# Attention and spectral mixing on one core: a head in halves, GpSimd's products tied to places on VectorE, two more packs of scores off ScalarE

## The chip, the core and the metric

The kernel runs on one core of a Trainium2 chip. The core has five engines that run side by side, each with its own in-order queue: TensorE (PE in the profile, weight loads PEld), VectorE (DVE), ScalarE (ACT), GpSimd (POOL) and SyncE (SP, which here only issues DMAs). They tell each other by semaphores when a buffer is written or free. The metric is the device time of one execution in microseconds (us).

## The reference

```python
def reference(A_x, A_wqkv, A_wo, B_x, B_w_r, B_w_i, gate_w):
    x = A_x                                                # 1 x 2048 x 448, bf16
    g = _sigmoid((x * gate_w).sum(-1, keepdims=True))
    a = _A_ref(x, A_wqkv, A_wo)                            # softmax attention, 16 heads of 28
    b = _B_ref(x, B_w_r, B_w_i)                            # irfft2(rfft2(x) * (w_r + i w_i))
    return g * a + (1 - g) * b
```

Attention needs 16 x 2048 x 2048 exponentials. The two-dimensional Fourier transforms are done as matmuls with constant matrices, in stages between which the data pass through DMAs.

## The kernel before

**Work units.** Heads go in four groups T of four. Queries go in chunks of 512: chunk c = 4T + qc, 16 in all. For one chunk, 16 key tiles i of 128 rows and 4 heads make 64 score tiles of 128 x 512, 1024 in the whole kernel. A score tile is one matmul on a strip of 32 rows of TensorE (`score`, L759).

**Two ways to an exponential.** Most score tiles go to ScalarE: TensorE writes three of them into the three-bank buffer ps3 or two into ps2, alternately, and one ACTIVATE (`exp`, L951) makes the exponentials of the whole buffer. The others are taken in packs of four heads of one (c, i) by VectorE (`pack_step`, L769, and `chain`, L781). Four evictions (L775) bring the scores from a background bank bg0 or bg1 to SBUF as 16-bit whole numbers, and a chain of seven operations o1 to o7 of 128 x 2048 elements (L789 to L810) builds the bits of the exponential. There are 28 packs. `away` (L914) decides before each score tile whether a step of a pack fits; `claim` (L995) picks the pack.

**Values and chunks.** `pv` (L871, matmuls L876) multiplies exponentials with values into one accumulating bank, psPV. When a chunk is complete, `close_chunk` (L833) copies the bank (L838), sends the row of sums through DMAs (r16), takes its reciprocal (L848), multiplies by the gate (L849), writes it to DRAM (rD), and reads it back spread over the partitions (rep). Then `scale` (L863) lets GpSimd multiply: the product at L867 writes a quarter of oT[T]. There are 15 such products; the last chunk is finished in `finale`.

**Background units.** Everything else is cut into units (projections of q and k, values, the Fourier stages, output blocks), each with one or more phases: matmuls into bg0 or bg1, then VectorE's eviction. `plan` (L958) writes a list of them with due times: `first` at once, `order` at BEGIN + GAP x n. The units for group T > 0 project q and k (`qk_unit`, L493); VectorE copies a quarter (L501) and squares it (L505), and the squares are summed by head for the softmax bound (`kn_unit`, `qn_unit`).

**The order.** The program is laid out by hand: `stream` steps through exponentials and keeps an estimate of each engine's time (`tp` TensorE, `tv` VectorE, `tg` GpSimd, `ta` ScalarE, with the constants E_... at the top). Before each exponential it lets values, units and pack steps in as far as the estimate has room (`step`, L1065; `dve`, L349; `fill_v`, L817, takes chain operations from the queue `vq`). It also adds matmuls on zeros (`zero`, `dummy`, L1134 and L1143, and L909) so that TensorE stays busy. What comes out is a fixed order on each engine; nothing is decided while it runs.

**Head and tail.** `head` (L281) transposes the first block of x (L278, copies L313, L315, L316), projects k and q of its 512 columns (L270), squares them on ScalarE (L298), subtracts half the squared norm by a matmul (L303) and copies them to kT and qT (L324, L325). It also transposes and copies block 1 and half of block 2 (L321, L327, L329). `first_unit` (L534) does the other three blocks of group 0 in the stream. `finale` (L1272 on) transposes the last chunk's sums (L1291), scales (L1292 to L1294), transposes back (L1295), multiplies by Wo (L1298) and adds what was kept of the other terms, on VectorE (L755) and ScalarE (L1304), with the f32 identity matmul (L1285) where ScalarE copies.

Of the kernel before, what the change touches and what calls it, by code (L numbers as in the profile page):

```python
# [16 lines left out]
ALU = mybir.AluOpType  # L17
# [30 lines left out]
GAP = 2.3  # L48
WINDOW, PULL = 3.4, 3900
READY = 1.2  # L50
NPT = 4
# [3 lines left out]
STEPS = 3400  # L55
BEGIN = 25.0

# [87 lines left out]
class Kernel:  # L145
    def __init__(self, ctx, tc, A_x, A_wqkv, A_wo, B_w_r, B_w_i, gate_w, out):
        self.ctx, self.tc = ctx, tc
        self.nc = tc.nc
        self.x = A_x[0]
        self.wqkv, self.wo, self.w_r, self.w_i = A_wqkv, A_wo, B_w_r, B_w_i  # L150
        self.gate_w = gate_w
        self.outv = out[0].rearrange("(p t) d -> p t d", t=NT)
        self.tp = self.tv = self.tg = self.ta = self.lock = 0.0
        self.gq, self.last_v = [], None
        self.bank_free = [0.0, 0.0]
        self.vq = []
        self.events = []
        self.marks = {}
        self.active = []
        self.cols = [0, 0, 0]  # L160


    def setup(self):
# [20 lines left out]
        for b in range(4):  # L184
            nc.sync.dma_start(out=self.xtok[:, 4 * b:4 * b + 4, :], in_=xv[:, 4 * b:4 * b + 4, :])
            if b == 0:

                for part, queue in ((1, nc.scalar), (0, nc.sync)):
# [16 lines left out]
        for q in (1, 0):  # L205
# [61 lines left out]
    def project(self, ps, T, q, b, pad=True):  # L267
        for c in range(4):
# [12 lines left out]
    def head(self):  # L281

        nc, tc = self.nc, self.tc
        with tc.tile_pool(name="hps", bufs=1, space=PSUM) as hp:
            def zeros(n):
                wt = hp.tile([P, 512], F32, name="wt", tag="wt")
# [3 lines left out]
            def turn(b, c0):  # L290
                pt = banks[b, c0]
                self.transposes(pt, b, c0)
                return pt

            def proj(q):
                self.project(pk[q], 0, q, 0, False)
                sq = self.rot2.tile([P, 512], BF16, name="sqh")
                nc.scalar.activation(out=sq[:], in_=pk[q][:], func=ACT.Square)  # L298
                return pk[q], sq

            def norm(q, pk, sq):
                off = 0 if q else KR
                nc.tensor.matmul(pk[:], lhsT=self.Sel[:, off:off + P], rhs=sq[:], start=False, stop=True,  # L303
                                 skip_group_check=True)


            banks = {(2, 0): hp.tile([P, 2, 512], BF16, name="t20")}
            zeros(8)
            banks |= {(0, c): hp.tile([P, 2, 512], BF16, name=f"t0{c}") for c in (0, 2)}
            pk = [hp.tile([P, 512], F32, name=f"pk{q}") for q in (0, 1)]  # L310
            banks |= {(1, c): hp.tile([P, 2, 512], BF16, name=f"t1{c}") for c in (0, 2)}
            pt = turn(0, 0)
            nc.vector.tensor_copy(out=self.xT[0:DC, 0:2, 0:512], in_=pt[0:DC])  # L313
            pt = turn(0, 2)
            nc.scalar.copy(out=self.xT[0:DC, 2, 0:512], in_=pt[0:DC, 0])  # L315
            nc.vector.tensor_copy(out=self.xT[0:DC, 3, 0:512], in_=pt[0:DC, 1])  # L316
            zeros(4)
            k = proj(1)
            q = proj(0)
            pt = turn(1, 0)  # L320
            nc.vector.tensor_copy(out=self.xT[0:DC, 0:2, 512:1024], in_=pt[0:DC])  # L321
            norm(1, *k)
            norm(0, *q)
            nc.vector.tensor_copy(out=self.kT[0][:, 0:512], in_=k[0][:])  # L324
            nc.scalar.copy(out=self.qT[0][:, 0:512], in_=q[0][:])  # L325
            pt = turn(1, 2)
            nc.vector.tensor_copy(out=self.xT[0:DC, 2:4, 512:1024], in_=pt[0:DC])  # L327
            pt = turn(2, 0)
            nc.vector.tensor_copy(out=self.xT[0:DC, 0:2, 1024:1536], in_=pt[0:DC])  # L329
            self.tv = 1.4  # L330
# [18 lines left out]
    def dve(self, cost, fast=False, at=0.0, of=None):  # L349


        start = max(self.tv, at)
# [140 lines left out]
    def qk_unit(self, T, q, b):  # L493
# [5 lines left out]
        def ve(ps):  # L499
            dst = (self.kT if q else self.qT)[T][:, 512 * b:512 * b + 512]  # L500
            nc.vector.tensor_copy(out=dst, in_=ps[:])  # L501
            if b == 0:
                self.sq = self.rot1.tile([P, S], BF16, name="sq")
                self.marks[f"sq{T}{q}"] = self.sq
            nc.vector.tensor_tensor(out=self.sq[:, 512 * b:512 * b + 512], in0=dst, in1=dst, op=ALU.mult)  # L505
            self.marks[f"sqt{T}{q}"] = self.dve(0.46, True) + 0.1
# [27 lines left out]
    def first_unit(self, q, b):  # L534
# [4 lines left out]
        def pe(ps):  # L539
            self.project(ps, 0, q, b, False)  # L540
# [14 lines left out]
        needs = ([f"T{b}.0", f"T{b}.2"] if b > 1 else []) if q else [f"W{b}"]  # L555
        return Unit(f"{'qk'[q]}0.{b}", [(pe, 0.96, 2048, ve, 1.06), (pe2, 0.30, 512, ve2, 0.60)], needs=needs)
# [224 lines left out]
    def chain(self, c, i, t16):  # L781
        nc = self.nc
        v = nc.vector
        st = {}
# [38 lines left out]

    def at(self, t, fn):
# [8 lines left out]
    def close_chunk(self, c):  # L833
# [23 lines left out]
        def spread():  # L857
# [3 lines left out]
            self.at(self.tv + 3.0, scale)  # L861

        def scale():  # L863
# [3 lines left out]
            nc.gpsimd.tensor_tensor(out=self.oT[T][:, QW * qc:QW * qc + QW], in0=o32[:], in1=st["rep"][:], op=ALU.mult)  # L867
            self.gp(1.27, self.tp + 0.1, lambda end: self.marks.update({f"oT{c}": end + 0.1}))
# [10 lines left out]
    def scores(self, k, end):  # L879
# [3 lines left out]
        t = self.tiles[k]  # L883
        start = max(self.tp, end + AP)
# [29 lines left out]
    def away(self, start, strips):  # L914
        if len(self.vq) > 8 or self.tv > start + 1.2:
# [10 lines left out]
        ps = self.psp.tile([P, 512], F32, name=f"bg{b}", tag=f"bg{b}", bufs=1)  # L926
        if self.tv < self.tp:
# [30 lines left out]
    def plan(self):  # L958
# [10 lines left out]
        def mix(a, b):  # L969
# [13 lines left out]
        T = {2: [self.turn_unit(2, 2)], 3: [self.turn_unit(3, c) for c in (0, 2)]}  # L983
        self.marks["T2.0"] = self.tv
        first = ([self.first_unit(1, 1)] + T[2] + [self.first_unit(1, 2)] + T[3] + [self.first_unit(1, 3)]
                 + [self.ek_unit()] + W[:2] + [self.first_unit(0, 1)] + W[2:])
        order = self.gate_unit() + [self.first_unit(0, 2), self.first_unit(0, 3)]
        order += mix(V, qk(1)) + mix(fA[:26], qk(2)) + fA[26:] + mix(BI[:22], qk(3)) + BI[22:] + Z
        order += [self.base_unit(t) for t in range(8, 16)]

        m = [(0.0, u) for u in first] + [(BEGIN + GAP * n, u) for n, u in enumerate(order)]
        m += [(0.0, self.out_unit(t)) for t in range(8)] + [(0.0, self.fin_unit(t)) for t in range(8, 12)]
# [47 lines left out]
    def pick(self):  # L1040
# [4 lines left out]
        banks = [b for b in (0, 1) if b not in self.open]  # L1045
# [12 lines left out]
    def ready(self):  # L1058

        t = [self.bank_free[b] for b in self.open]  # L1060
        if len(self.open) < 2 and self.mand:
            t.append(max([self.marks.get(n, 1e9) for n in self.mand[0][1].needs] + [self.tp]))
        return min(t, default=1e9)

    def step(self, u, b, limit):  # L1065
# [5 lines left out]
        if b not in self.open:  # L1071
            self.take(u)
            self.open[b] = u, self.psp.tile([P, 512], F32, name=f"bg{b}", tag=f"bg{b}", bufs=1)
        ps = self.open[b][1]
        n = len(self.vq)
        self.fill_v(start + cost + PV - 0.3)
# [9 lines left out]
        if not u.phases:  # L1086
            del self.open[b]
            self.marks[u.name] = max(self.tv, self.tp) + u.lag
# [48 lines left out]

    def dummy(self):


        while sum(self.cols) < STEPS:
            if self.pv_open:
                self.nc.tensor.matmul(self.psPV[:], lhsT=self.warm[:], rhs=with_free(self.warm[:], [[0, 4], [1, P]]), start=False, stop=False,  # L1143
                                      skip_group_check=True)
                self.add(self.tp + E_MM, 512)
                self.dummies += 1
            elif self.pv_c < NC and self.tp >= self.pv_free:
                self.zero(self.psPV, self.tp)
            else:
                b = [i for i in (0, 1) if self.bank_free[i] <= self.tp and i not in self.open]  # L1150
                if b:
                    ps = self.psp.tile([P, 512], F32, name=f"bg{b[0]}", tag=f"bg{b[0]}", bufs=1)
# [214 lines left out]
```

## Time and profile before

| | |
|---|---|
| median of 3 runs | 439.64 us (439.36 to 439.95) |
| profiled execution | 441.74 us, span of its instructions 439.7 us |
| first exponential begins | 10.58 us |
| last exponential ends | 430.67 us |
| TensorE busy (with modelled ends) | 407.9 us, 93% |
| VectorE busy | 391.4 us, 89% |
| ScalarE busy | 419.7 us, 95% |
| GpSimd busy | 29.9 us, 7% |

A line of a group reads: line of the code, engine, operation, what it writes <- what it reads, shapes, count | busy us, mean ns of one | idle time of the engine before them and what ended it. A line of the timeline reads: start, us, engine, line, operation, count, and in brackets the idle time before it and what ended that. A line of the windows reads: stretch, its length, then for PE, PEld, DVE, ACT and POOL the busy us and the number of instructions, then the granted clock of TensorE as a share, the DMA share and GB/s. Operations of one engine overlap at their ends, so the distance of two starts is less than the duration of one.

### The profile page before, as it was taken

The numbers are of one execution on the slowest core, as the hardware profiler recorded it, in microseconds if no ns is written. First come the engines' busy times: TensorE is split into PE (matmuls) and PEld (weight loads), VectorE is DVE, ScalarE is ACT, GpSimd is POOL, SyncE is SP. The second block draws the span as 40 slices with busy tenths as digits, with TensorE's granted clock in tenths as the row PEclk, the third lists the DMA queues.
The fourth block names the chain that finished last, engine by engine and source line by source line (L and its number), as shares of the span: only waits on it lengthen the run. The fifth ranks groups of instructions, "written<-read, shape, count | busy, mean of one in ns | idle before, by whom it ended". The sixth has DMA issues, their size and how long they took to land.

```text
span 439.7 us, 8021 instructions
## 1 busy us (share of the span) xinstructions
PE 407.9 (93%) x3114; PEld 148.0 (34%) x3114; DVE 391.4 (89%) x614; ACT 419.7 (95%) x375; POOL 29.9 (7%) x33
## 2 busy tenths in 40 slices
PE   8888999999999999999999999899998899999995
PEld 4433332333333333333333333333443333333321
DVE  5686997999778999999999899999999989999953
ACT  3998998999999999999999999999999999999992
POOL 6000001100001000010110101001010101002010
PEclk9999998999999999999999999999999999999999
DMA  9900100000002010221432235024320000010111
GB/s 233 207 9 1 6 27 1 26 1 26 3 13 54 15 47 22 73 65 35 112 95 79 53 65 92 16 43 93 87 94 4 26 1 26 12 36 33 37 64 42
DMA packets 24597, 21.69 MB, mean 49 GB/s; under 512 B 10256, under 2 KB 20240, under 8 KB 24528
## 3 DMA queue, kind: packets, MB, share of 16 engines
q1 hardware_dynamic: 23808, 20.86, 19.3%
q8 instruction: 24, 0.39, 0.4%
q10 hardware_dynamic: 752, 0.33, 0.3%
q14 instruction: 13, 0.11, 0.1%
HBM read 15.36 MB, written 1.97 MB: 39 GB/s over the span
## 4 chain that ended last, share of the span: by engine, by line
ACT 38%; PE 24%; DVE 20%; issue 13%; DMA 4%; POOL 0%; SPq 0%; ACTq 0%; DVEq 0%; POOLq 0%
ACT Pt L951 38%; PE psPV L876 5%; PE ps L761 4%; DVE t L775 3%; PE bg L909 3%; PE bg L270 2%; DVE n L806 2%; PE bg L761 2%; DVE pa L800 2%; DVE pa L803 1%; DVE pa L797 1%; DMA Wv<-in_gate_w_dram 1%; PE psPV L1143 1%; DMA W<-in_A_wqkv_dram 1%; DVE U L620 1%
## 5 line engine op out<-in xcount | busy, mean ns | idle before, releaser
L951 ACT ACTIVATE Pt<-ps 128x1536 bf16<-128x1536 f32 x347 | 394.6, 1312 | 4.9 <-PE ps L761 4.6
L761 PE MATMUL ps<-qT,kT 32*128 32x512 bf16 x912 | 145.3, 382 | 10.6 <-ACT Pt L951 8.1
L876 PE MATMUL psPV<-Pt,vsb 128*32 128x512 bf16 x868 | 86.1, 388 | 0.0
L761 PEld LDWEIGHTS <-kT 32*128 32x128 bf16 x1024 | 50.3, 91 | 102.6 <-issue 95.4
L775 DVE TENSOR_SCALAR t<-bg 128x512 uint16<-128x512 f32 x112 | 76.3, 683 | 4.9 <-PE ps L761 3.9
L909 PE MATMUL bg<-warm 32*128 32x512 bf16 x145 | 55.5, 383 | 3.6 <-DVE t L775 1.3
L867 POOL TENSOR_TENSOR oT<-o,rep 128x512 bf16<-128x512 f32 x15 | 21.2, 1416 | 389.8 <-DMA rep<-rD 303.1
L761 PE MATMUL bg<-qT,kT 32*128 32x512 bf16 x112 | 42.7, 381 | 4.9 <-DVE base L741 1.1
L876 PEld LDWEIGHTS <-vsb 128*32 128x32 bf16 x1024 | 23.9, 93 | 54.8 <-issue 50.9
L806 DVE TENSOR_TENSOR n<-t,pa 128x2048 uint16<-128x2048 uint16 x28 | 36.1, 1288 | 0.4
L803 DVE TENSOR_TENSOR pa<-pa,n 128x2048 f16<-128x2048 f16 x28 | 35.5, 1267 | 0.6
L797 DVE TENSOR_TENSOR pa<-pa,n 128x2048 f16<-128x2048 f16 x28 | 34.7, 1238 | 0.1
L270 PE MATMUL bg<-xT,Wg 128*128 128x512 bf16 (+1 forms) x120 | 31.8, 388 | 0.6 <-DVE t L775 0.3
L909 PEld LDWEIGHTS <-warm 32*128 32x128 bf16 x145 | 12.3, 91 | 39.3 <-issue 38.7
L800 DVE TENSOR_SCALAR pa<-pa 128x2048 f16<-128x2048 f16 x28 | 22.9, 818 | 0.2
L620 DVE CAST U<-bg 128x450 bf16<-128x450 f32 x32 | 19.8, 621 | 2.0 <-PE bg L632 1.2
L793 DVE TENSOR_SCALAR pa<-n 128x2048 f16<-128x2048 uint16 x28 | 20.6, 737 | 0.1
L789 DVE TENSOR_SCALAR n<-t 128x2048 uint16<-128x2048 uint16 x28 | 19.7, 703 | 0.3
L810 DVE TENSOR_SCALAR Pd<-n 128x2048 uint16<-128x2048 uint16 x28 | 19.5, 696 | 0.2
L1143 PE MATMUL psPV<-warm 128*128 128x512 bf16 x58 | 19.4, 386 | 0.0
L270 PEld LDWEIGHTS <-Wg 128*128 128x128 bf16 (+1 forms) x128 | 10.9, 98 | 15.8 <-issue 7.9
L609 PE MATMUL bg<-Bd,xT 128*128 128x450 bf16 x64 | 15.0, 356 | 0.1
(159 smaller groups left out, 406.3 us busy)
## 6 DMA issues: line engine op xcount, KB each, us to landing
rep<-rD SPq DMA_DIRECT2D x15, 256.0 KB
CR<-cRB SPq DMA_DIRECT2D x8, 256.0 KB
UT<-U SPq DMA_DIRECT2D x16, 112.5 KB
VT<-U SPq DMA_DIRECT2D x16, 112.5 KB
xtok<-in_A_x_dram SPq DMA_DIRECT2D x4, 448.0 KB
CR<-cCS SPq DMA_DIRECT2D x8, 192.0 KB
Wqkv<-in_A_wqkv_dram SPq DMA_DIRECT2D x1, 1176.0 KB
Wri<-in_B_w_r_dram SPq DMA_DIRECT2D x8, 112.5 KB
```

Of the source, the lines that this page charges most:

```text
L270: self.nc.tensor.matmul(ps[:], lhsT=self.Wg[T, q][0:k, c, :], rhs=self.xT[0:k, c, 512 * b:512 * b + 512], start=(c == 0), stop=(c == 3))
L620: self.nc.vector.tensor_copy(out=U[:], in_=ps[:, 0:F2])
L761: self.nc.tensor.matmul(out, lhsT=self.kT[T][32 * h:32 * h + 32, 128 * i:128 * i + 128], rhs=self.qT[T][32 * h:32 * h + 32, QW * qc:QW * q ...
L775: nc.vector.tensor_scalar(out=pk["t"][:, h, :], in0=ps[:], scalar1=SCALE * LOG2E * 512.0, scalar2=127.0 * 512.0, op0=ALU.mult, op1=ALU.add)
L797: v.tensor_tensor(out=st["a"][:], in0=st["a"][:], in1=st["n"][:], op=ALU.mult)
L800: v.tensor_scalar(out=st["a"][:], in0=st["a"][:], scalar1=k, scalar2=C1 * k, op0=ALU.mult, op1=ALU.add)
L803: v.tensor_tensor(out=st["a"][:], in0=st["a"][:], in1=st["n"][:], op=ALU.mult)
L806: v.tensor_tensor(out=st["n"][:], in0=t16[:], in1=st["a"][:], op=ALU.add)
L876: self.nc.tensor.matmul(self.psPV[32 * h:32 * h + 32, :], lhsT=self.vsb[:, i, 4 * T + h, :], rhs=pcs[h], start=first, stop=last, tile_posi ...
L909: self.nc.tensor.matmul(ps[:], lhsT=self.warm[sl], rhs=with_free(self.warm[sl], [[0, 4], [1, P]]), start=True, stop=True, tile_position=(3 ...
L951: self.nc.scalar.activation(out=Pt[:, 0:n, :], in_=ps[:, 0:n, :], func=ACT.Exp, scale=SCALE)
L1143: self.nc.tensor.matmul(self.psPV[:], lhsT=self.warm[:], rhs=with_free(self.warm[:], [[0, 4], [1, P]]), start=False, stop=False, skip_grou ...
```

## The change

- The head works on two halves of 256 columns for q and k. All four squares are of 256 columns, three on ScalarE and one on VectorE; ScalarE copies one half of q, VectorE the other and both halves of k. VectorE makes both copies of the first block of x. Of block 1 only one half is transposed in the head, and none of block 2; the rest become units of the stream. The loads and spreadings of the first q and k weights change places.
- The order of the first units is a written list, FIRSTS; the projections of `first_unit` are two phases. Until unit W0 begins, psPV's bank serves as a third bank for units. Waits of TensorE's estimated time are filled with matmuls on zeros (`until`, `one_zero`).
- The squares of a group's q or k are one operation of 128 x 2048 at the fourth quarter, put at the front of the queue, instead of four of 128 x 512.
- A product of GpSimd is no longer issued when its estimated time comes, but put on a list, 8 us (estimated) behind the load of rep. `dve` takes it from the list when the next operation that is not of the queue, with the wait before it, is estimated at 1.0 us or more, when the queue is empty, or after 8 us. A memset by VectorE of a corner of the product's output, just ahead of that operation, holds the product until then.
- When three or fewer key tiles of the chunk under way are left, the chain operations of that chunk's packs are all done at once (`hurry`).
- GAP is 2.35 instead of 2.3; the first 8 value units are mixed with the second group's q and k, and the other 8 with the units that follow.
- In the finale the scaling and the transposing back go in two halves, three of the four blocks are copied by ScalarE, one by VectorE, and two DMAs move to SP.
- By the order of the built programs, the number of packs becomes 30 instead of 28 and the number of exponentials on ScalarE 362 instead of 365.

```diff
-GAP = 2.3
+GAP = 2.35
+BESIDE = 1.0
+NV, NBASE = 8, 8
+MOST = 8
+LATE = 3
+FIRSTS = "T1.2 k0.1 T2.0 T2.2 k0.2 T3.0 T3.2 k0.3 ek0 W0 q0.1 W1 W2 W3"
...
     def head(self):
...
-            pt = turn(0, 0)
-            nc.vector.tensor_copy(out=self.xT[0:DC, 0:2, 0:512], in_=pt[0:DC])
-            pt = turn(0, 2)
-            nc.scalar.copy(out=self.xT[0:DC, 2, 0:512], in_=pt[0:DC, 0])
-            nc.vector.tensor_copy(out=self.xT[0:DC, 3, 0:512], in_=pt[0:DC, 1])
-            zeros(4)
-            k = proj(1)
-            q = proj(0)
...
+            self.transposes(pt[0], 0, 0)
+            nc.vector.tensor_copy(out=self.xT[0:DC, 0:2, 0:512], in_=pt[0][0:DC])
+            self.transposes(pt[1], 0, 2)
+            nc.vector.tensor_copy(out=self.xT[0:DC, 2:4, 0:512], in_=pt[1][0:DC])
+            zeros(1)
+            ka = (bank("wt"), 1, 0)
+            for part in ((0, 1), (2, 3)):
+                for piece in (qa, qb, ka):
+                    proj(piece, part)
+            sa, sb = square(qa, nc.scalar), square(qb, nc.scalar)
+            proj(kb, (0, 1))
+            norm(qa, sa)
+            norm(qb, sb)
+            sk = square(ka, nc.vector)
+            proj(kb, (2, 3))
+            done(qa, nc.scalar.copy)
+            done(qb, nc.vector.tensor_copy)
+            norm(ka, sk)
+            sk = square(kb, nc.scalar)
+            done(ka, nc.vector.tensor_copy)
+            self.transposes(pt1, 1, 0)
+            norm(kb, sk)
+            nc.vector.tensor_copy(out=self.xT[0:DC, 0:2, 512:1024], in_=pt1[0:DC])
+            done(kb, nc.vector.tensor_copy)
...
     def dve(self, cost, fast=False, at=0.0, of=None):
+        if self.jobs and not fast:
+            since, job = self.jobs[0]
+            if not self.vq or max(at - self.tv, 0.0) + cost >= BESIDE or self.tv > since + 8.0:
+                self.jobs.pop(0)
+                job()
...
-            if b == 0:
-                self.sq = self.rot1.tile([P, S], BF16, name="sq")
-            nc.vector.tensor_tensor(out=self.sq[:, 512 * b:512 * b + 512], in0=dst, in1=dst, op=ALU.mult)
+            if b == 3:
+                self.vq.insert(0, (squares, E_TT, None))
...
+    def hurry(self):
+        if self.pv_c < NC and len(self.left[self.pv_c]) <= LATE:
+            self.fill_v(1e9, max((j + 1 for j, (_, _, of) in enumerate(self.vq) if of and of["c"] == self.pv_c), default=0))
...
-            self.at(self.tv + 3.0, scale)
+            self.at(self.tv + 8.0, lambda: self.jobs.append((self.tv, scale)))
...
+            nc.vector.memset(o[0:32, 0:4], 0.0)
+            nc.gpsimd.tensor_tensor(out=o, in0=o32[:], in1=st["rep"][:], op=ALU.mult)
...
-        order += mix(V, qk(1)) + mix(fA[:26], qk(2)) + fA[26:] + mix(BI[:22], qk(3)) + BI[22:] + Z
+        order += mix(V[:NV], qk(1)) + mix(V[NV:] + fA[:26], qk(2)) + fA[26:] + mix(BI[:22], qk(3)) + BI[22:] + Z
...
-        banks = [b for b in (0, 1) if b not in self.open]
+        banks = [b for b in (0, 1, 2)[:2 if self.begun else 3] if b not in self.open]
...
+    def until(self, at):
+        while self.tp + E_MM <= at and sum(self.cols) < STEPS and self.one_zero():
+            self.tp += E_MM
+        self.tp = max(self.tp, at)
...
     def finale(self, psp):
...
-        pf = [r[3][:, 0], r[3][:, 1], r[3][:, 2], r[2][:, 0]]
+        pf = [r[3][:, 0], r[3][:, 1], r[2][:, 0], r[3][:, 2]]
...
-        v.tensor_tensor(out=z[:], in0=f[:], in1=with_free(i16[:], [[1, NT], [0, 32]]), op=ALU.mult)
-        v.transpose(out=self.oT[T][:, QW * qc:QW * qc + QW], in_=z[:].rearrange("p j r -> p (j r)"))
+        for a in (0, 8):
+            zh = z[:, a:a + 8, :]
+            v.tensor_tensor(out=zh, in0=f[:, a:a + 8, :], in1=with_free(i16[:, a:a + 8], [[1, 8], [0, 32]]), op=ALU.mult)
+            v.transpose(out=self.oT[T][:, QW * qc + 32 * a:QW * qc + 32 * a + 256], in_=zh.rearrange("p j r -> p (j r)"))
+            for e in (a // 4, a // 4 + 1):
...
+        for e in (0, 1, 3):
             t = 4 * qc + e
...
+            fin = self.rot3.tile([P, F2], BF16, name="X1")
+            nc.scalar.copy(out=fin[:, 0:D], in_=pf[e][:, 0:D])
+            (nc.scalar if e == 3 else nc.sync).dma_start(out=self.outv[:, t, :], in_=fin[:, 0:D])
+        self.add_base(pf[2], 4 * qc + 2, nc.sync)
```

## The prediction

> **What bounds the kernel now.** I read the page first: busy time by engine, the clock row, the costliest groups.
>
> ```profile
> span 439.7 us, 8021 instructions
> ...
> PE 407.9 (93%) x3114; PEld 148.0 (34%) x3114; DVE 391.4 (89%) x614; ACT 419.7 (95%) x375; POOL 29.9 (7%) x33
> ...
> L951 ACT ACTIVATE Pt<-ps 128x1536 bf16<-128x1536 f32 x347 | 394.6, 1312 | 4.9 <-PE ps L761 4.6
> ```
>
> ScalarE's exponentials (L951) fill nine tenths of the span. The next view is ScalarE's timeline, merged; it shows where they do not run.
>
> ```profile
> 10.58 6.88 ACT L951 ACTIVATE early<-ps 128x1536 bf16<-128x1536 f32 x6 [0.68 <-PE ps L761]
> ...
> 39.61 2.37 ACT L951 ACTIVATE Pt<-ps 128x1536 bf16<-128x1536 f32 x2 [1.06 <-PE ps L761]
> ...
> 70.96 1.45 ACT L951 ACTIVATE Pt<-ps 128x1536 bf16<-128x1536 f32 x1 [1.34 <-PE ps L761]
> 73.12 123.61 ACT L951 ACTIVATE Pt<-ps 128x1024 bf16<-128x1024 f32 x109 [0.71 <-PE ps L761]
> ```
>
> The first exponential begins at 10.58, the last ends at 430.67, and 9.03 us of tail follow. Between, ScalarE waits four times before 43 us (0.18, 0.20, 1.06, 0.26) and twice around 70 us (1.34, 0.71); afterwards 109 of them run without a gap. So time is gained by (a) an earlier first exponential, (b) fewer of them, (c) fewer of those waits, (d) a shorter tail. What VectorE and TensorE do counts only where ScalarE waits for it.
>
> The groups with shapes kept apart give the prices.
>
> ```profile
> L951 ACT ACTIVATE Pt<-ps 128x1536 bf16<-128x1536 f32 x174 | 265.2, 1524 | 3.6 <-PE ps L761 3.6
> L951 ACT ACTIVATE Pt<-ps 128x1024 bf16<-128x1024 f32 x173 | 189.7, 1099 | 1.2 <-PE ps L761 1.0
> L800 DVE TENSOR_SCALAR pa<-pa 128x2048 f16<-128x2048 f16 x28 | 22.9, 818 | 0.2
> ```
>
> **(b) Fewer exponentials: -3.6 us.** The built order of the changed program has 120 evictions of scores to VectorE instead of 112 (30 packs, not 28), so 904 score tiles of 512 are left to ScalarE instead of 912: 173 + 8 three-wide, 170 + 10 two-wide and a single, against 174 + 8, 173 + 10. Instructions overlap, so I price by starts: 109 in 123.61 us (55 two-wide, 54 three-wide) are 2.27 us a pair. The third tile costs 1524 - 1099 = 0.425; so two-wide 0.92, three-wide 1.345, a single 0.50. 3 x 0.92 + 1.345 - 0.50 = 3.6.
>
> **What it costs VectorE.** A pack: four evictions that start 0.60 apart and seven operations whose means (703, 737, 1238, 818, 1267, 1288, 696 ns) less 0.08 overlap each sum to 6.2: 8.6 us, two are 17. Squares: 24 pieces of 0.425 go, each held up 0.08 by the copy just before; six whole ones come, of which no row exists; the nearest (L797, two half-width inputs, same size) is 1.24. 24 x 0.43 - 6 x 1.24 = 2.9 saved (0 if a whole one cost four pieces); I take 2. Fifteen small memsets at 0.06 (the row of L253): +1. Then GpSimd's products. The timeline around 66 us shows what they do now:
>
> ```profile
> 66.12 1.27 POOL L867 TENSOR_TENSOR oT<-o,rep 128x512 bf16<-128x512 f32 x1 [56.50 <-DMA rep<-rD]
> 66.31 1.62 DVE L793 TENSOR_SCALAR pa<-n 128x2048 f16<-128x2048 uint16 x1
> ...
> 68.59 1.59 PE L1134 MATMUL bg<-warm 128*128 128x512 bf16 x3 [0.46 <-DVE t L775]
> ```
>
> L793, which alone takes 0.68 (the same kind at 64.46), takes 1.62 when a product began 0.19 before it, and ends 0.54 behind it. Over the chain's groups the means exceed the undisturbed 0.68 and 1.22 by 218 and 142 ns in all, times 28: 10 us. In the changed order a product waits for a memset, and in all 15 places VectorE's next operation reads PSUM (0.6 us, in five places 1.1 or more) and only then a chain operation follows. The products come later (planned 8 us behind the issue of rep instead of 3), but each still stands ahead of the next chunk's reciprocal, so SP's next load of the single rep buffer doesn't wait for it. I count half of the 10 as gone (bounds: none, all). Net for VectorE: +17 - 2 + 1 - 5 = +11.
> [...]
>
> Is there room? By windows VectorE is busy 42.5, 49.2, 48.9, 48.1, 47.9, 47.6 us in the six 50 us stages from 100 on, and 63.7 of 72 between 28 and 100: 24 us idle from 28 to 400. With +11 some 13 are left, less the 3.6 by which the time shrinks. The packs go where room is: in the old order one eviction stands between score tiles 200 and 250, in the new one 8, since the keys and queries of the second group now mix with 8 value units, not 16. **New waits of ScalarE: +1.5 us.** Bounds: 0 (in 150 to 200 VectorE is busy 98.4% and ScalarE idle 0.30), and +2.3 if all stages came to the worst of those six (250 to 300, idle 0.55: 6 x 0.55 = 3.3 against 1.6 now, and 8/6 of the difference for 28 to 430); I take a value nearer the upper end, since every stage is now about as full as the fullest were.
>
> **(a) The head: -0.95 us.** Now, from the timeline: second half of xT copied by 6.71, eight projections 6.32 to 8.22, squares from 7.39 and 8.26 (0.60 each), copies 9.31 to 9.99, scores 10.11, exponential 10.58. In halves: VectorE's two xT copies start 5.21 and 5.81 and end 5.90 and 6.50 (no wait for ScalarE's copy). Six half-width matmuls at 0.12 (1.90/8, halved) from 5.97, six more until 7.4. ScalarE squares q from 7.1, half of 0.60 plus what is fixed, 0.38 each. VectorE takes the first keys at 7.6: copy 0.42, wait 0.1, product 0.29, to 8.3 or 8.4; norm matmul to 8.6; copy 0.42 to 9.05; scores 9.15, exponential 9.6. Behind the norm of the first keys on TensorE stand 8 transposes (0.61) and the last norm, ahead of the scores; they end about 9.15 too. Their input is there: now they run at 8.06. Bounds: -0.3 (a half as dear as a whole on VectorE: +0.7), -1.1.
>
> **(c) Early waits: -1.3 us.** The 1.06 at 38.5 is for qT of the second chunk (TensorE waits for DVE qT L554, 38.36 to 39.05). In the new order that copy stands behind two operations of the first chain and one value unit, not seven and three: some 5.7 + 1.5 us of VectorE's work come after it instead. Moved in return: transposes and copies of the second block (two of 0.69) into the stream; a third PSUM bank takes them and the next keys are wanted only 16 tiles (7.3 us) after the first exponential. Bounds: 0, -1.7.
>
> **(c) The half clock: -1.0 us.** The windows on both sides of 69.13 us:
>
> ```profile
> 65.72:69.13 3.41, 2.79 (x20) 0.88 (x20) 3.27 (x6) 3.41 (x4) 1.27 (x1) 1.00 0.00 0
> 69.13:72.54 3.41, 3.30 (x10) 0.64 (x8) 1.14 (x2) 1.94 (x2) 0.00 (x0) 0.50 0.02 2
> ```
>
> TensorE (first busy column) had 2.79 of 3.41 us, with the wait of 0.46 behind VectorE's late eviction; then its clock is 0.50 for 3.41 us and ScalarE waits 1.34 + 0.71 = 2.05. It began with the product of 66.12. With products moved I count half (0 to -2.05).
> [...]
>
> **(d) The tail: -0.5 us.**
>
> ```profile
> 433.13 0.71 DVE L1295 STREAM_TRANSPOSE oT<-oz 128x512 bf16<-128x512 bf16 x1
> ...
> 434.68 0.62 DVE L755 TENSOR_TENSOR U<-ps,late 128x448 bf16<-128x448 f32 x1 [0.84 <-PE ps L1298]
> 435.33 0.53 ACT L1304 CAST X<-ps 128x448 bf16<-128x448 f32 x1 [4.66 <-DVE U L755]
> ```
>
> Four copies alternate between two engines, each waiting for the other, 434.68 to 436.84. The halves (0.42 + 0.43 each) give the first part of oT at 433.3 but the second at 434.1, 0.25 later than now; TensorE has a third f32 matmul (0.88) for two fills fewer and is free at 433.9 either way. ScalarE's first copy waits for the last of the four matmuls (the order's semaphore values), so starts at 434.9; three copies 0.45 apart end at 436.35. Their first two DMAs go from SP (0.35 each), ahead of VectorE's. Bounds: 0, -1.0.
>
> Later places of units (GAP 2.35, out units), the hurried chains and the reversed weight loads have one answer: nothing waits for them in rows of before (q and k weights land together, 4.98 and on), 0. The last product stands 11 score tiles before the end (before: 26, at 420.75) with its four units behind it; late by 1 us it would stall the last scores by as much, inside the +1.5.
>
> Sum: -3.6 - 0.95 - 1.3 - 1.0 - 0.5 + 1.5 = -5.85. The profiled execution took 441.74 (span 439.7 and 2.0 around it), so 435.9 for its like; the median shown is 439.64, so **433.8**. A difference under 0.2% (0.9 us) can't be told from none.
>
> **Rivals.**
> A. No half clock, no early and no new wait: -3.6 - 0.95 - 1.7 - 2.05 - 0.5 = -8.8, **430.8**. For it: the causes are removed. Against: 97% of VectorE's time is taken.
> B. Products don't begin at the chosen places: a memset may run when the landing of rep has not come, and the product falls into chain operations as before. VectorE keeps its 10 us and the clock its 2.05: about +1.0 and +0.5, **435.3**. For: landing of rD has taken 3.7 us in the chain of waits; against: the product is placed 8 us behind the issue of rep.
> C. VectorE becomes the bound: both packs dearer than its idle time; ends and early waits are all that is left: **437**. Against: 24 us idle.
> D. Slower: half-clock windows. Place: the fuller stages, where a late eviction holds TensorE's queue as at 68.59. Price 2.05 each; it decides from four more than I count (-5.85 + 4 x 2.05 = +2.35): **442.0**. For: TensorE's fill matmuls fall from 237 to 230, and VectorE has less slack to catch up. Against: one in 365 us now, with worse stalls.
>
> **How the numbers follow.** Forecast 0.58 (its own range 431.8 to 436), A 0.17, B 0.11, C 0.08, D 0.06. The range 430.6 to 437.4 leaves out D and some edges of A and C. Faster: all but D and the edge of C, 0.91; within 0.2% 0.03; slower 0.06.
>
> **What would show it.** First exponential at 9.6; 362 exponentials; no gap near 38; chain operations without 1.6 to 2.2 us runs; clock row without a half window before the tail; last exponential to end of span 8.5. I am wrong if ScalarE's idle time between 100 and 400 us exceeds 3.3, if a half window stays, or if the first exponential is later than 10.2.

## The result and the profile after

The changed kernel takes 436.6 us (median of 9 runs, 434.45 to 439.07); the kernel before, beside it, 439.9 us (9 runs, 439.35 to 440.75). The ratio is 0.9926, 95% interval 0.9908 to 0.9943: faster by 0.7%, inside the range, 2.8 us above the 433.8 forecast. Its runs also spread more than before's. The profiled execution took 436.6 us. In what follows, runs that lie over 1.5% above the fastest of their kernel are left out (two of the twelve of experiment 3).

Page of the changed kernel: span, busy time, largest group.

```profile
span 434.6 us, 8031 instructions
...
PE 402.0 (93%) x3100; PEld 148.3 (34%) x3119; DVE 399.9 (92%) x638; ACT 415.4 (96%) x373; POOL 27.7 (6%) x33
...
L1002 ACT ACTIVATE Pt<-ps 128x1536 bf16<-128x1536 f32 x344 | 391.0, 1312 | 4.1 <-PE ps L798 2.7
```

VectorE gained 8.5 us (11 were forecast), ScalarE lost 4.3. An exponential is as long as before on average (1312 ns); there are 362. ScalarE's timeline, merged as before:

```profile
10.24 7.16 ACT L1002 ACTIVATE early<-ps 128x1536 bf16<-128x1536 f32 x6 [0.93 <-PE ps L798]
...
24.93 3.71 ACT L1002 ACTIVATE early<-ps 128x1536 bf16<-128x1536 f32 x3 [0.60 <-PE ps L798]
...
37.07 2.40 ACT L1002 ACTIVATE Pt<-ps 128x1536 bf16<-128x1536 f32 x2 [0.60 <-PE ps L798]
40.61 4.62 ACT L1002 ACTIVATE Pt<-ps 128x1536 bf16<-128x1536 f32 x4 [1.15 <-PE pv L923]
...
76.25 140.53 ACT L1002 ACTIVATE Pt<-ps 128x1024 bf16<-128x1024 f32 x124 [0.19 <-PE ps L798]
217.20 96.16 ACT L1002 ACTIVATE Pt<-ps 128x1024 bf16<-128x1024 f32 x85 [0.43 <-PE ps L798]
313.58 2.45 ACT L1002 ACTIVATE Pt<-ps 128x1536 bf16<-128x1536 f32 x2 [0.23 <-PE ps L798]
317.07 11.48 ACT L1002 ACTIVATE Pt<-ps 128x1536 bf16<-128x1536 f32 x10 [1.04 <-PE ps L798]
```

From 76 us on ScalarE hardly stops: 209 exponentials with one wait between them. But the first begins at 10.24, not 9.6; the early waits are 0.15, 0.60, 0.60 and 1.15 where before has 0.18, 0.20, 1.06 and 0.26; and there is again a gap that belongs to a stretch of half clock (the granted clock of TensorE is 0.50 there), now near 315 (before: near 70). Windows of the changed kernel (busy us and count of PE, PEld, DVE, ACT, POOL, then the granted clock):

```profile
310.32:313.74 3.42, 2.06 (x24) 0.58 (x22) 3.42 (x6) 3.19 (x4) 0.00 (x0) 1.00 0.15 37
313.74:317.15 3.41, 3.41 (x20) 0.83 (x17) 3.31 (x4) 2.37 (x3) 0.00 (x0) 0.50 0.45 145
```

TensorE had 2.06 of 3.42 us to do while VectorE was busy throughout; then the clock is 0.50 for 3.41 us. The tail:

```profile
428.33 0.45 DVE L1369 STREAM_TRANSPOSE oT<-oz 128x256 bf16<-128x256 bf16 x1
...
429.11 0.45 DVE L1369 STREAM_TRANSPOSE oT<-oz 128x256 bf16<-128x256 bf16 x1
430.07 0.62 DVE L792 TENSOR_TENSOR U<-ps,late 128x448 bf16<-128x448 f32 x1 [0.52 <-PE ps L1372]
```

After it ScalarE copies three blocks in one piece, 430.26 to 431.66; last exponential to end of span is 8.43 us (before 9.04).

### The profile page after: what moved, and what is told of

Its sections match the earlier page's. It is cut to its first block, busy times and chain, and to the rows that moved or that the text cites. A ratio compares the mean times of both kernels' runs of the same rounds, so it can differ in the third digit from the quotient of the medians.

```text
span 434.6 us, 8031 instructions
## 1 busy us (share of the span) xinstructions
PE 402.0 (93%) x3100; PEld 148.3 (34%) x3119; DVE 399.9 (92%) x638; ACT 415.4 (96%) x373; POOL 27.7 (6%) x33
## 4 chain that ended last, share of the span: by engine, by line
ACT 36%; PE 34%; DVE 15%; issue 12%; DMA 1%; SPq 0%; DVEq 0%; ACTq 0%
ACT Pt L1002 36%; PE psPV L923 6%; PE ps L798 5%; PE bg L959 5%; DVE t L812 3%; PE bg L276 2%; PE bg L798 2%; PE psPV L1203 2%; DVE pa L834 1%; DMA Wri<-in_B_w_i_dram 1%; PE bg L755 1%; PE bg L751 1%; DVE pa L830 1%; PE wt L297 1%; DVE kT L535 1%
## 5 line engine op out<-in xcount | busy, mean ns | idle before, releaser
L1002 ACT ACTIVATE Pt<-ps 128x1536 bf16<-128x1536 f32 x344 | 391.0, 1312 | 4.1 <-PE ps L798 2.7
L812 DVE TENSOR_SCALAR t<-bg 128x512 uint16<-128x512 f32 x120 | 82.0, 683 | 4.3 <-PE bg L798 2.1
L959 PE MATMUL bg<-warm 32*128 32x512 bf16 x150 | 57.7, 385 | 6.6 <-DVE t L812 3.4
L798 PE MATMUL bg<-qT,kT 32*128 32x512 bf16 x120 | 45.9, 383 | 2.5 <-DVE t L812 0.9
L912 POOL TENSOR_TENSOR oT<-o,rep 128x512 bf16<-128x512 f32 x15 | 19.0, 1269 | 391.7 <-DVE oT L911 299.4
L843 DVE TENSOR_TENSOR n<-t,pa 128x2048 uint16<-128x2048 uint16 x30 | 38.1, 1270 | 0.3
L834 DVE TENSOR_TENSOR pa<-pa,n 128x2048 f16<-128x2048 f16 x30 | 37.2, 1240 | 0.1
L840 DVE TENSOR_TENSOR pa<-pa,n 128x2048 f16<-128x2048 f16 x30 | 36.6, 1221 | 0.3
L276 PE MATMUL bg<-xT,Wg 128*128 128x512 bf16 (+1 forms) x98 | 28.8, 380 | 1.4 <-issue 0.3
L830 DVE TENSOR_SCALAR pa<-n 128x2048 f16<-128x2048 uint16 x30 | 21.3, 710 | 0.1
L837 DVE TENSOR_SCALAR pa<-pa 128x2048 f16<-128x2048 f16 x30 | 20.7, 690 | 0.3
L1002 ACT ACTIVATE early<-ps 128x1024 bf16<-128x1024 f32 (+1 forms) x12 | 13.9, 1209 | 1.7 <-PE ps L798 1.5
```

The source lines that it names most:

```text
L276: self.nc.tensor.matmul(ps[:], lhsT=self.Wg[T, q][0:k, c, :], rhs=self.xT[0:k, c, 512 * b:512 * b + 512], start=(c == 0), stop=(c == 3))
L798: self.nc.tensor.matmul(out, lhsT=self.kT[T][32 * h:32 * h + 32, 128 * i:128 * i + 128], rhs=self.qT[T][32 * h:32 * h + 32, QW * qc:QW * q ...
L812: nc.vector.tensor_scalar(out=pk["t"][:, h, :], in0=ps[:], scalar1=SCALE * LOG2E * 512.0, scalar2=127.0 * 512.0, op0=ALU.mult, op1=ALU.add)
L830: v.tensor_scalar(out=st["a"][:], in0=st["n"][:], scalar1=C3 * k * k, scalar2=C2 * k, op0=ALU.mult, op1=ALU.add)
L834: v.tensor_tensor(out=st["a"][:], in0=st["a"][:], in1=st["n"][:], op=ALU.mult)
L840: v.tensor_tensor(out=st["a"][:], in0=st["a"][:], in1=st["n"][:], op=ALU.mult)
```

## Theories and experiments

**H, half clock.** The gain is what was summed, 5 us, and stretches at half clock take part of it back, more often than before. **V, VectorE.** At 92% busy it is late everywhere, and the clock only shows it. Each run's mean granted clock is known, so the two can be told apart. Ratios below are to the kernel before on the same chip, with 95% intervals.

**1. The changed kernel again** (no edit).

> The changed kernel itself, once more. Theory H (half clock): what the change gained is 5.2 us (434.5 at a mean granted clock of 0.999), and each stretch of 3.41 us at half clock, which is 0.004 of the mean clock, takes 1.5 us of it back (435.3 and 435.4 at 0.996, 439.07 at 0.987 in the runs of the result); so each run here lies within 0.5 us of 434.4 + 375 x (0.999 - clock), and the median is about 436.5. Rival V (VectorE): the missing 2.8 us is late evictions of VectorE, now 92% busy, in every run; then the times spread without following the clock, and the one at 0.999 was luck.

435.74 us (6 runs; 0.991, 0.989 to 0.9931). Each run is within 0.6 us of the expected line; 0.5 was expected, and two of the six lie just outside it. The median is 0.8 under the expected 436.5, at a mean clock of 0.9948 (0.9933 in the first nine runs). A line through the 15 runs of both comparisons gives 434.0 at full clock and 1.47 us more for each 0.0039 of mean clock (one half window of 3.41 in 434); correlation 0.93. Through 39 runs of before it gives 439.4 (1.1 per window, correlation weaker), so at full clock the change is worth 5.3 us. Mean clock: before 0.9974, after 0.9939, about 0.9 windows more. This profiled execution had no half window (a step of 3.41 us at half clock) before the tail: span 432.8 against 434.6. H holds for the spread.

**2. The new finale alone**, on the kernel before: scaling and transposing back in two halves, three blocks copied by ScalarE.

```diff
+        for a in (0, 8):
...
+        for e in (0, 1, 3):
```

> The kernel before with the new finale alone (last copies on ScalarE and VectorE), the order of all the rest as before. The prediction's 0.5 us and the 0.6 that the two traces show from the last exponential to the end (9.03 to 8.44): 0.5 to 0.6 us under before, a ratio of 0.9987. Rival: the copies were covered by the last DMA's issue, and the tail got shorter by the order of the last stores; then within 0.2 us of before.

440.07 us (0.9994, 0.9978 to 1.001): the times of 12 runs with a spread of 2 us cannot tell theory and rival apart. The trace can: last exponential to last copy is 6.16 us in before, 5.53 here and 5.51 in the changed kernel, so 0.63 is the finale's; the wait for the last DMA behind it varied (2.88, 3.22, 2.92), so here only 0.3 of it reached the end of the span. This profile has no half window in the middle and serves below as the undisturbed picture of the old order.

**3. Products when rep has landed.**

```diff
-            nc.vector.memset(o[0:32, 0:4], 0.0)
```

> The changed kernel without the VectorE memset that GpSimd's product waits for: a product begins as soon as its strip has landed, wherever VectorE is then. [...] Rival V: VectorE is the bound, the 5 us of excess come out in the time, 2 to 4 us slower than the changed kernel.

440.66 us (median of ten runs; 1.0035, 1.0004 to 1.0066), 5 us above the changed kernel. Its line: 437.9 at full clock, 1.32 per window, mean clock 0.9896. So 3.9 us are lost at full clock and about 1.2 through the clock: that VectorE has slack for the ungated products and the time rises by 0 to 1 us, as H had it, fell. The 3.9 lies in V's 2 to 4, but V's reason is not right either: VectorE's excess grows by 2.8 us only (below). GpSimd's timeline of this run, then of the changed kernel:

```profile
70.91 1.79 POOL L911 TENSOR_TENSOR oT<-o,rep 128x512 bf16<-128x512 f32 x1 [61.36 <-DMA rep<-rD]
...
136.51 1.65 POOL L911 TENSOR_TENSOR oT<-o,rep 128x512 bf16<-128x512 f32 x1 [20.72 <-DMA rep<-rD]
```

```profile
94.56 1.27 POOL L912 TENSOR_TENSOR oT<-o,rep 128x512 bf16<-128x512 f32 x1 [9.53 <-DVE oT L911]
...
149.58 1.26 POOL L912 TENSOR_TENSOR oT<-o,rep 128x512 bf16<-128x512 f32 x1 [33.90 <-DVE oT L911]
```

The ungated products fall into chain operations and are held up themselves: 1587 ns on average, 1269 in the changed kernel. Above the undisturbed 0.68 and 1.22 the chain's group means exceed by 229 ns in all x 30 = 6.9 us here, 4.1 in the changed kernel (forecast 5), 10 in before. ScalarE's waits from 50 to 425 us, the ungated run and then run 1 (columns: total, times, longest):

```profile
ACT Pt L1001 <- PE ps L798: 2.8, 7, 1.0
```

```profile
ACT Pt L1002 <- PE ps L798: 0.8, 3, 0.3
```

VectorE's excess is 2.8 us larger and ScalarE's later waits 2.0, of which 1.0 falls into a half window at 221 us. One place shows how the rest can come about: behind the product at 136.51 the chain operation L843 takes 2.18 us (1.22 undisturbed), the eviction of kT after it starts at 139.16, TensorE waits 0.60 for that eviction, and ScalarE 0.28 at 141.5, where run 1 has no wait. That it goes like this at every place is not shown, and these waits do not add up to the 3.9. The gate works, and is worth more than the whole change shows.

**4. Every strip fill on all 128 rows.**

```diff
-   lhsT=self.warm[sl], rhs=with_free(self.warm[sl], [[0, 4], [1, P]]), ..., tile_position=(32 * s, 0)
+   lhsT=self.warm[:], rhs=with_free(self.warm[:], [[0, 4], [1, P]])
```

> The changed kernel with every fill matmul on all 128 rows instead of on one strip of 32, the same count, order and columns; only a discarded result differs. Theory H: TensorE's activity in the windows that came before half clock (0.33 to 0.37 by rows, columns and time) rises above 0.37 all over, the half windows go away, the granted clock is 0.998 or more in nearly all runs, and the median is 434.4 to 435.0 with a spread under 1 us. Rival V: the clock is a symptom, the spread and the median (436.6) stay within 0.5 us; third way: full rows can't run beside other strips, so TensorE is later for the scores and the time rises by over 1 us.

449.27 us (1.0213, 1.019 to 1.0237): the third way. 13 us for 150 fills, 0.09 each; TensorE's busy time rises from 402 to 423, by 21 us of the 32 that 150 fills come to at 0.213 each (measured below). By this estimate, on a strip most of a fill had run beside other work; in the changed kernel a fill and three scores start together at 12.29. Whether the fills themselves take the time or the changes between strips and the whole array, this run does not separate. The mean clock did rise, to 0.9968 (5 runs).

**5. The old head** with the rest as the change has it (functions of before, FIRSTS without T1.2 and T2.0).

> The changed kernel with the head of the kernel before (pieces of 512 columns, key piece first, T1.2 and T2.0 in the head), the rest of the order as the planner then gives it (30 packs, 362 exponentials). By the first runs the changed kernel takes 434.0 us at full clock and 1.47 us more for each 0.0039 of mean granted clock; its mean clock is 0.994, that of before 0.998. Theory X (the new head and the order that follows it leave TensorE too little to do between 20 and 27 us): the clock returns to 0.997 or 0.998, and the time is 434.0 plus the 0.35 to 0.95 us that the new head saves plus at most one half window in two, 434.5 to 435.7, faster than the changed kernel's 436.1. Rival Y (the half windows come from the rest of the changed order, such as the one at 313.7 us): the clock stays at 0.994 and the time is 436.5 to 437.2.

438.13 us (11 runs; 0.9935, 0.9913 to 0.9957), mean clock 0.9929; line: 434.8 at full clock. Y holds for the clock: it does not come back, and the profile's half windows lie at 215.6 and 321.4 us. The time is 0.9 above what Y gave. At full clock the new head is worth 0.8 by the two lines (434.8 - 434.0).

**6. q0.1 ahead of ek0.**

```diff
-FIRSTS = "T1.2 k0.1 T2.0 T2.2 k0.2 T3.0 T3.2 k0.3 ek0 W0 q0.1 W1 W2 W3"
+FIRSTS = "T1.2 k0.1 T2.0 T2.2 k0.2 T3.0 T3.2 k0.3 q0.1 ek0 W0 W1 W2 W3"
```

> The changed kernel with the one entry q0.1 of its list moved ahead of ek0: VectorE then evicts W1 behind one chain operation where the changed kernel has it behind three. Theory: ScalarE's waits at 37.0 and 40.5 us (0.60 and 1.15) came from the evictions of W1 and W2 that stand behind chain operations; the 0.60 goes, early waits fall from 2.35 to between 1.2 and 1.8 us, and the time by 0.5 to 1.2 us at the same clock. Rival: the late one is then W0, W2 or q0.1 itself; early waits stay within 0.4 of 2.35 or grow, the time too.

435.42 us (0.989, 0.9865 to 0.9915). First the changed kernel's VectorE and TensorE where it waits:

```profile
33.30 1.22 DVE L834 TENSOR_TENSOR pa<-pa,n 128x2048 f16<-128x2048 f16 x1
34.55 0.69 DVE L837 TENSOR_SCALAR pa<-pa 128x2048 f16<-128x2048 f16 x1
35.16 0.62 DVE L412 TENSOR_TENSOR vsb<-bg,ek 128x448 bf16<-128x448 f32 x1
```

```profile
35.83 0.39 PE L923 MATMUL pv<-oT,vsb 128*32 128x512 bf16 x2 [0.74 <-DVE vsb L412]
```

W1's eviction stands behind three chain operations (L830, L834, L837); TensorE's queue holds at the values (0.74 us), and the scores behind them start at 36.60, ScalarE's next exponential at 37.07. In run 6 the eviction runs at 31.88, and ScalarE's timeline there is

```profile
33.25 4.62 ACT L1002 ACTIVATE Pt<-ps 128x1536 bf16<-128x1536 f32 x4
38.84 2.36 ACT L1002 ACTIVATE Pt<-ps 128x1536 bf16<-128x1536 f32 x2 [0.96 <-PE ps L798]
```

The waits at 37 and at 24.9 are gone (the second was not forecast), one of 0.96 stays, behind the eviction of W2: the theory holds for W1. By this run's line it takes 433.6 at full clock, 0.5 under the changed kernel, the low end of the 0.5 to 1.2 expected.

**7. Without the planner's full fills in its first 30 us** (9 or 10 matmuls).

```diff
-        self.nc.tensor.matmul(ps[:], lhsT=self.warm[:], ...)
+        at < 30.0 or self.nc.tensor.matmul(ps[:], lhsT=self.warm[:], ...)
```

> The changed kernel without the 9 or 10 full fill matmuls that the planner puts into the first 30 us of its own time (they only write a bank that is overwritten). Two of them, 0.81 us, stand ahead of the scores whose exponential waits 0.61 us at 24.3. Theory X: the wait goes (0.6 us), but TensorE's activity in the windows from 17 to 30 us falls below the 0.36 by rows, columns and time, so nearly every run has one or two half windows more there, the mean clock falls to 0.990 or lower, and the time is 436.5 to 439. Rival: the wait itself lowered the activity; without it the clock is the same or higher and the time 435.0 to 435.7.

436.58 us (0.9913, 0.9888 to 0.9939), mean clock 0.9883, and the profile has half clock from 25.7 to 32.6: theory X. What the two fills cost ScalarE (0.6) the ten early fills give back in clock.

**8. Without the 150 strip fills.**

> The changed kernel without the 150 strip fills (32 rows of the array, 512 columns, a result that nothing reads), 57.7 us of TensorE's busy time in all. If the throttle counts busy time, the activity of the busy share falls by a tenth and half windows are many: mean clock under 0.98, time over 441. If it counts rows and columns, 150 strip fills are 8 us of 434, so a clock of 0.99 or more, and a time between 434.5 and 438. Rival: the fills cost time beside the scores, and without them the time falls under 434.

437.08 us (0.992, 0.9897 to 0.9943), mean clock 0.9882: between the two, nearer to rows and columns. Ten microseconds at half clock from 214.5 in its profile, the place of runs 3, 5, 6 and 7.

**Where the weak places are.** I counted TensorE's activity in each execution: every matmul's columns at 0.213 us per 512 (in the head of the changed kernel, before its clock rose, seven fills in a row span 3.19 us and one 0.63: 0.427 from start to start, twice 0.213; at full clock four span 1.04 and one 0.39: 0.217), times its share of the array's rows and columns. In the traces of before and after, half clock lasts 3.413 us in the middle, and the clock changes at whole steps of that length from the moment it first rose (before: 4.28 + 19 x 3.413 = 69.13; after: 6.54 + 90 x 3.413 = 313.7), a moment that differs from execution to execution (4.93 in run 1, 3.65 in run 10). Over any 3.413 us, before has one place under 0.36 (66 us: 0.35). The changed kernel has three: 23 us (0.26), 212 us (0.25) and 311 us (0.27; 0.40 in run 1). In this execution the clock stayed at 1.00 over the first two and went to 0.50 after the third. That it depends on how the steps fall on a place, and that the spread comes from this, is my estimate from these counts. SP's queue and TensorE of the changed kernel at the second place:

```profile
208.34 0.62 SPq L658 DMA_DIRECT2D UT<-U  x1
209.02 0.45 SPq L694 DMA_DIRECT2D CR<-cCS  x1
209.52 0.42 SPq L699 DMA_DIRECT2D Wri<-in_B_w_r_dram  x1
209.99 0.43 SPq L700 DMA_DIRECT2D Wri<-in_B_w_i_dram  x1
```

```profile
215.85 0.35 PE L710 MATMUL bg<-UT,CR 128*128 128x450 bf16 x1 [0.89 <-DMA Wri<-in_B_w_i_dram]
```

The last piece of UT is followed at once by 417 KB of constants for a later unit; from 210 to 213 us the DMA engines' busy share is 1.00 to 1.06. In before those were issued at 212.82, behind a rep that waited 3.1 us for the landing of rD.

**9. These constants at A.10.**

```diff
-            for g in ((0, 2) if stage in "AI" else (g,)):
+            for g in ({"A": (0, 2, 4), "I": (0, 2)}.get(stage) or (g,)):
...
-            if stage in "BZ" and g % 2:
+            if stage in "BZ" and g % 2 or u.name == "B.0":
```

> The changed kernel with the third pair of constants of stage B (CR, Wri, 417 KB) loaded at unit A.10 with the first two pairs, instead of at B.0, where SP issues it right behind the last transposing transfer UT<-U. Counted over any 3.41 us, TensorE's activity (rows, columns, time) has three weak places in the changed kernel, 0.26 at 23 us, 0.25 to 0.27 at 212 us and 0.27 to 0.40 at 311 us, where before has one of 0.35. Theory: the 417 KB share the DMA engines with UT<-U, so the first product of B waits until 215.65 (0.80 of it TensorE's whole queue), and that makes the weak place at 212. Then this kernel's first product of B comes 1 to 2 us earlier, the place rises over 0.36, the mean clock over the runs goes from 0.994 to 0.996 and the median from 436.1 to 435.2 to 435.6. Rival: UT<-U is late by itself; the place stays under 0.3, clock and time stay.

435.01 us (0.988, 0.9856 to 0.9904), mean clock 0.9965. SP issues nothing for 7 us behind UT, and TensorE finds its data there when ScalarE lets it go on:

```profile
211.03 0.62 SPq L658 DMA_DIRECT2D UT<-U  x1
218.54 0.33 SPq L694 DMA_DIRECT2D CR<-cCS  x1
```

```profile
217.24 0.40 PE L798 MATMUL ps<-qT,kT 32*128 32x512 bf16 x3 [0.31 <-ACT Pt L1002]
217.57 0.36 PE L710 MATMUL bg<-UT,CR 128*128 128x450 bf16 x1
```

(This execution's exponentials run 2.8 us behind run 1's, from a half clock at 26 us, so the product comes 0.8 us earlier than run 1's 215.65; 1 to 2 were expected.) The lowest activity near 212 us is now over 0.41, so the theory holds for this execution. It is not the whole cause, as run 10 shows.

**10. Edits 6 and 9 together.**

> q0.1 ahead of ek0 (the sixth run's edit) and the constants at A.10. Two of the three weak places are gone then. Theory: the two gains add, mean clock 0.996 or 0.997, median 434.0 to 434.8. Rival: as the sixth run, 435.4.

433.57 us (4 runs, 433.07 to 433.93; 0.9856, 0.9833 to 0.9879), mean clock 0.9985, spread under 1 us: all four runs lie under all 15 of the changed kernel and under the expected 434.0. That is more than the two gains added, by less than their intervals. But the two places are raised and not gone: the lowest activity is 0.35 at 23 us (run 6 has the same) and 0.34 at 210 us. TensorE's first product of B here:

```profile
213.22 0.35 PE L710 MATMUL bg<-UT,CR 128*128 128x450 bf16 x1 [0.30 <-DMA UT<-U]
```

Where ScalarE is not late, as it was in run 9's execution, the product waits for UT itself. From the issue of UT's last piece to the product it is 6.9 us here and 7.4 to 7.9 in runs 1 and 6 and the changed kernel, so the constants cost 0.5 to 1.0 us of it: run 9's theory and its rival are both right in part.

**11. And four buffers for U.**

```diff
-        U = self.rot3.tile([P, F2], BF16, name="U")
+        U = self.rot4.tile([P, F2], BF16, name="U")
```

> The same with four buffers instead of three for the tiles U, whose transfers VectorE waited for (0.86 us) ahead of the half window at 313.7, and two instead of three for the last output tile. Theory: the third weak place goes as well; the mean clock is 0.997 or 0.998 as before's, and the time 433.0 to 434.0, below both kernels. Rival: the place at 311 to 325 has another cause (VectorE's chain), and this is no faster than the run beside it within 0.3 us.

433.36 us (0.9855, 0.9833 to 0.9876), mean clock 0.998: the fastest median, below both kernels, but within 0.3 us of run 10, as the rival had it. VectorE's wait ahead of the third place in the changed kernel,

```profile
308.19 0.63 DVE L657 CAST U<-bg 128x450 bf16<-128x450 f32 x1 [0.86 <-DMA VT<-U]
```

is gone in its trace. Run 10, with three buffers, still has such a wait (0.70 at 305.73), and its third place is not weak (0.39). So the buffers are not shown to be the cause. In the changed kernel TensorE then waits 1.36 us, to 313.07, for VectorE's evictions among chain operations; why that happens in one execution and not in run 1 stays open.

## Why the prediction came out 2.8 us off

Between first and last exponential I split the span into ScalarE's idle time before 50 us, after it, and the rest.

| term | predicted | measured | from |
|---|---|---|---|
| fewer exponentials | -3.6 | -3.7 | rest: 414.8 to 411.1 |
| head | -0.95 | -0.8 to -1.2 | first exponential at like clock |
| early waits | -1.3 | +0.8 to +1.1 | 1.70 to 2.50 and, run 1, 2.84 |
| half clock | -1.0 | +1.3 | 0.9 windows x 1.47 |
| tail | -0.5 | -0.6 | 9.04 to 8.43 |
| new waits | +1.5 | -0.5 | runs 2 and 1, after 50 us: 1.49 to 0.95 |
| sum | -5.85 | -3.2 to -3.9 | medians -3.3 and -4.1 |

Of the three signs of being wrong that the prediction names, two came: a half window stayed, and the first exponential began at 10.24.

**Right.** The price of the exponentials, the tail, VectorE's load, the gate of the products (half of the chain's excess) came out as said, each within 0.2 us or, for the two on VectorE, within 2.5. At one place the operation that covers a product was short, and the next one still paid: L843 at 84.03 takes 2.08 behind a product that began at 83.77, under a 0.69 us eviction. **The head** was right too, though the profile seems to say otherwise: "wrong if the first exponential is later than 10.2", and it began at 10.24. TensorE's first transposes, in the changed kernel and in run 10:

```profile
4.38 1.94 PE L284 MATMUL t<-ident,xtok 128*112 128x128 bf16 x16
```

```profile
4.64 1.10 PE L284 MATMUL t<-ident,xtok 128*112 128x128 bf16 x16 [0.45 <-DMA xtok<-in_A_x_dram]
```

The clock rose at 6.54 us in the one and 3.65 in the other, and run 10's first exponential starts at 9.77. At an early rise the old head gives 10.58 (4.28) and the new one 9.80 (4.93); at a late one 11.47 (6.41) and 10.24 (6.54).

**Wrong: the early waits, -1.3.** "Moved in return" I counted only transposes of the second block. The wait for q0.1 did go; but q0.1 ahead of W1, W2 means those stand behind the first chain, and TensorE's in-order queue holds the scores behind their values (0.74 us at 35.83). Run 6 takes 1.3 of it out (2.50 to 1.19) by one place in the list. At the wait of 24.9 two fills and a pack step stand on one bank one after the other, ahead of the scores; without the fills (run 7) that wait is gone.

**Wrong: the half clock, -1.0.** I took the half window of the one profiled execution (441.74, 2.1 over the median) for part of the kernel; 33 of before's 39 runs have a mean clock of 0.996 or more, so there was little to remove. And the change makes new weak places, by the order of the first units (run 6: 0.26 to 0.35 at 23 us) and in part by another load order on SP (runs 9 and 10); the cause of the third stays open. This was rival D's mechanism with one window, not four; its reasons (fewer fills, less slack) did not name the DMA.

**Wrong: the new waits, +1.5.** VectorE busy for 98.4% of a stage did not make ScalarE wait more, as the row I set aside (before, 150 to 200 us, idle 0.30) already said; behind a held-up operation it waited 0.28 us at one place of run 3.

Errors of +2.2, +2.3 and -2.0 make the 2.8 with the small rest. So it is partly luck that the time fell as near as it did: the new waits that did not come hid 2.0 of the 4.5 us by which the early waits and the clock were misjudged. What stays open: the sum at full clock (-4.5 to -5.2 by this table) is less than the two lines give (-5.3), by no more than before's weak line may be off.

## What to carry to other kernels

Ask of a stall in the one profiled execution whether the median runs have it at all; their mean granted clock tells. When a unit is moved up an in-order queue, price what now stands behind it on every queue, SP's included, and who is blocked by that: here one place in a list held 1.3 us of ScalarE's early waits (run 6). Before a tuned kernel is packed tighter, look for the places where the filler engine is thin. In the changed kernel the one at 311 us (activity 0.27) cost ScalarE a wait of 0.23 us there, and in the 3.41 us at a clock of 0.50 that followed one of 1.04.

## What was not expected of the hardware

In the 13 profiled executions, 12 steps of 3.413 us before the tail preceded a fall to half clock from full. Eleven had an activity of 0.19 to 0.36 by the count above (highest 0.36); no step that kept the clock had less than 0.365. The exception (0.384) is run 4, whose fills are all on 128 rows. Busy time alone does not separate them: before fell after a step with 2.79 of 3.41 us busy, and run 1 kept the clock after one with 2.31 of 3.41 (213.14 to 216.55 us). Nor was TensorE idle ahead of a fall: it was busy in 2.06 of the 3.42 us in the changed kernel, in 2.56 of 3.40 in run 3. Share of the array times time separates the steps of these executions, all but one. The 0.36 was named (run 7's expectation) before runs 5 to 11 were made and sorts their seven falls, but the gap is narrow. That the chip counts just that is not shown: leaving out the strip fills (run 8) is 8 us of activity by it, and cost as much clock (mean 0.9882) as leaving out ten full fills at one weak place (run 7, 0.9883).
